# A 94-row table load becomes a 96-row load in a Fourier-mixing and MLP kernel

## The chip, the core and the metric

The kernel runs on one core of a Trainium2 chip. The metric is the device time of one execution in microseconds (us). The kernel before took 1952.17 us, the median of 8 runs (1951.83 to 1952.98). A profile is one further execution, with its own time and its own span (first to last recorded instruction).

## The reference

The input x has 8 sequences of 3008 rows and 256 columns. The reference takes the discrete Fourier transform over both axes, keeps the real part, and sends each of the 24064 rows through an MLP without biases:

```
X = fft(fft(x, axis=1), axis=2).real          # 8 x 3008 x 256
h = X.reshape(24064, 256) @ w_in              # w_in: 256 x 2048
g = h * clip(h + 3, 0, 6) / 6
out = g @ w_out                               # w_out: 2048 x 256, float32 throughout
```

## The kernel before, in words

3008 = 47 x 64, so the transform along a sequence is done in two stages (47 points, then 64), and the one along the columns is folded into the first weight matrix. The 8 sequences are taken as 4 pairs. For each pair, stage 1 reads x in eight tiles of four n2-columns, writes z to DRAM, and stage 2 reads it back transposed as g (load_g, L310). The MLP then runs over all (pair, chunk, step) triples, with the stages of the next pair put between its steps. The first pair has nothing to run beside, so its stage 1 is the head of the program, and this is where the change lies.

The head, in the order in which each engine meets it:

- TensorE (PE) is given nine dummy matmuls on zeros, keep_awake(9) (L669), each run as two, before anything else; then, tile by tile, stage 1 and one more keep_awake.
- The DMA queue of SyncE (SP) carries, one after the other, FI (L670: 128 rows of 33 numbers, row indices and a sign), F0 (L671: 94 rows of 6 x 96 numbers, the six tables of the first pair's stage 1; 94 = 2 x 47, the two sequences of the pair stacked), and CE (L679: 128 rows of two times 128 numbers). Later it carries C, T and the stores of z.
- VectorE (DVE) turns the indices of FI into integers (IX, L676). ScalarE (ACT) casts CE to the 16-bit E (L681) and then clears parts of T by two wide copies from Z (L688), before it copies the first z out of PSUM (L268, L279).
- GpSimd (POOL) issues the loads of x: load_forward (L154 and, for the first tile only, also L156) brings 96 rows in, load_partners (L175) gathers the rows in reversed order with IX. Each such pair of loads is 768 KB. Three tiles are loaded ahead (xpool holds two of them, spool one).
- fold (L180 to L201) adds and subtracts the two on DVE and writes y, which has two buffers. stage1_first (L253) multiplies y by the tables in F0 on PE: L261 and L263 into pt, L272, L275 and L278 into ps. ACT copies the results to z, and SP stores 16 rows of z at once (L285); the other rows are kept in the list later and are stored during the first chunk.

The eight tiles are taken in the order 7, 0, 1, ... 6 (ORDER). The load of tile k + 3 stands in GpSimd's program after the fold of tile k, whose buffers it takes over:

```
for c in ORDER[0:3]:
    load_x(first, c)
for k, c in enumerate(ORDER):
    for part in range(2):
        fold(first, c, part, nc.vector)
    stage1_first(first, c)
    keep_awake(1)
    if k + 3 < NXC:
        load_x(first, ORDER[k + 3])
```

Behind the last x load GpSimd issues the first four pieces of the weights (load_w, L555), and, once g has landed (see, L723), four more. From then on exponent_a (L574), exponent_b (L586), mantissa (L597, L598) and join rebuild the weights, fold_w_in (L635, L643) multiplies the first matrix by the column transform, and the MLP begins with mlp1 (L379). The program's order is written by hand (manual_schedule); semaphores between the engines follow from the tiles.

F0 is a tile of apool (tag "a", four buffers), the pool which later holds the MLP's activations a. The load of x for the first pair already has 96 rows where 94 are used (PR0 + 2, L153).

Of the kernel before, what the change touches and what calls it, by code (L numbers as in the profile page):

```python
# [7 lines left out]
F32 = mybir.dt.float32  # L8
# [50 lines left out]
def kernel(  # L59
# [10 lines left out]
    nc = tc.nc  # L70
# [8 lines left out]
    PB, PZ = P // 2, 2 * NK1  # L79
    PX = PB + N1 + 1  # L80
    PR0, PZ0 = 2 * N1, 2 * PZ
# [19 lines left out]
    apool = ctx.enter_context(tc.tile_pool(name="apool", bufs=4))  # L101
# [11 lines left out]
    ctx.enter_context(tc.manual_schedule())  # L113

    F = consts.tile([P, 5 * PB], F32, name="F")
    F0 = apool.tile([PR0, 6 * PZ0], F32, tag="a", name="F0")
    FI = consts.tile([P, NP * NXC + 1], F32, name="FI")
    IX = consts.tile([P, NP * NXC], I32, name="IX")
    T = consts.tile([P, 2, NG, 2, 2 * KK, N2], F32, name="T")
# [89 lines left out]
    def bank(shape, name):  # L209
        if starting[0]:  # L210
            return ps_a.tile(shape, F32, tag="acc", name=name)
        return ps_d.tile(shape, F32, tag="d", name=name)
# [40 lines left out]
    def stage1_first(pr, c):  # L253
        y = pr.y.pop(c)
        n = XC if c < NXC - 1 else XC - 1

        def table0(i):
            return F0[:, i * PZ0:(i + 1) * PZ0]

        pt = ps_h.tile([P, 2 * TB], F32, tag="uv", name="pt")[0:PZ0]  # L260
        nc.tensor.matmul(pt[:, 0:n], table0(5), y[:, 0:n, P], start=True, stop=True)  # L261
        for k in range(2 if n < XC else 0):
            nc.tensor.matmul(pt[:, n:XC], table0(k + 1), y[:, n + k, P:P + 1], start=(k == 0), stop=(k == 1))  # L263

        k = ORDER.index(c)
        pool, tag = (zpool, "z") if k < 2 else (cpool, "c") if k < 5 else (qpool, "q") if k < 7 else (apool, "a")
        z = pool.tile([PZ0, XC, D + 1], F32, tag=tag, name="z")
        nc.scalar.copy(z[:, :, D], pt[:, 0:XC])  # L268
        for i in range(XC // 2):
            ps = bank([P, 2, D], "ps1")[0:PZ0]  # L270
            if (c, i) == (NXC - 1, XC // 2 - 1):
                nc.tensor.matmul(ps[:, 0], table0(0), y[:, 2 * i], start=True, stop=False, skip_group_check=True)  # L272
                for k, (j, cs) in enumerate([(XC - 1, slice(0, P + 1)), (XC, slice(0, P + 1)),
                                             (XC - 1, slice(P + 1, D)), (XC, slice(P + 1, D))]):
                    nc.tensor.matmul(ps[:, 1, cs], table0(k + 1), y[:, j, cs], start=False, stop=(k % 2 == 1),  # L275
                                     skip_group_check=True)
            else:
                nc.tensor.matmul(ps, table0(0), y[:, 2 * i:2 * i + 2, :], start=True, stop=True)  # L278
            nc.scalar.copy(z[:, 2 * i:2 * i + 2, 0:D], ps)  # L279
        if pr.zd is None:  # L280
            pr.zd = dpool.tile([NG, 2, 2 * KK, 2, NS, D + 1], F32, tag="zd0", name="zd")
        zd = pr.zd[:].rearrange("g b k c n d -> (g b k c) n d")[:, c * XC:(c + 1) * XC, :]

        n0 = PZ0 // NG
        nc.sync.dma_start(out=zd[0:n0], in_=z[0:n0])  # L285
        later.append((zd[n0:], z[n0:]))
# [381 lines left out]
    nc.vector.memset(ones[:], 1.0)  # L668
    keep_awake(9)  # L669
    nc.sync.dma_start(out=FI[:], in_=c_stage1[:, 5 * PB + 6 * PZ0:])  # L670
    nc.sync.dma_start(out=F0[:], in_=c_stage1[0:PR0, 5 * PB:5 * PB + 6 * PZ0])  # L671
    bias = wpool.tile([P, 2], F32, tag="bias", name="bias")
    for i in range(2):
        nc.vector.memset(bias[:, i:i + 1], (2 * i - 1) * 7.5 / 16.0 - 896.0)
# [331 lines left out]
```

## Time and profile before

| | |
|---|---|
| median of 8 runs | 1952.17 us (1951.83 to 1952.98) |
| the profiled execution | 1952.85 us, of it span 1950.8 us |
| mean clock granted to PE | 0.999 of full speed |
| PE busy | 1929.1 us (99% of the span) |
| HBM | 57.57 MB read, 37.32 MB written |
| queue q0 (issued by POOL) | 36.67 MB, 6.7% of 16 DMA engines' span |
| queue q1 (issued by SP) | 58.05 MB, 12.5% of 16 DMA engines' span |

How to read it: "busy" is the time in which an engine had an instruction running. A line of the chain of waits gives when a piece of the chain that ended last began, how long it took and what it was: an instruction with its source line, or a DMA that something waited for. A line of the waits gives who waited for whom, the total in us, how often, and the longest. "DMA share" is the mean busy share of the core's 16 DMA engines: 1 is all of them working, 0.125 is two of them. "Landing" is when the instruction that waits for a transfer may go on.

### The profile page before, as it was taken

To read this page: it belongs to the slowest core of one execution; us is meant where nothing else is said; L and a number is where in the kernel's file an instruction comes from. 1 tells how busy PE (TensorE), PEld (TensorE's weight loads), DVE (VectorE), ACT (ScalarE), POOL (GpSimd) and SP (SyncE) were. 2 spreads that over 40 slices of the span, in tenths; PEclk is the share of its full clock that TensorE was granted. 3 is DMA by queue.
4 is the path that set the end of the run, shared out by engine and by line. 5 is a ranking of instruction groups with operands and counts; after the bars stand their busy time and mean duration, and the time that the engine had idled before them with its cause. 6 is when DMAs were issued, how large, how long until landed. Compare 5 with 4: busy or idle time off the path is not lost.

```text
span 1950.8 us, 27925 instructions
## 1 busy us (share of the span) xinstructions
PE 1929.1 (99%) x9254; PEld 1658.6 (85%) x9254; DVE 1438.9 (74%) x2777; ACT 681.9 (35%) x1167; POOL 1416.0 (73%) x1620
## 2 busy tenths in 40 slices
PE   8999999999999999999999999999999999999997
PEld 3678888888998888888898888888899888888887
DVE  6787767777777777777787777777778777777777
ACT  4633333333333333333333333333333333333332
POOL 3168888886678887787678887878667667666765
PEclk9999999999999999999999999999999999999999
DMA  7531222211112122121111221212110101101000
GB/s 212 181 80 49 71 54 58 57 39 35 34 32 55 44 68 70 42 55 28 41 34 44 58 56 42 51 50 54 35 28 20 28 17 26 35 13 28 19 19 20
DMA packets 148943, 96.71 MB, mean 50 GB/s; under 512 B 117777, under 2 KB 131221, under 8 KB 148798
## 3 DMA queue, kind: packets, MB, share of 16 engines
q1 hardware_dynamic: 137334, 58.05, 12.5%
q0 software_dynamic: 10672, 36.67, 6.7%
q8 instruction: 73, 1.20, 0.3%
q14 instruction: 72, 0.59, 0.1%
q10 hardware_dynamic: 792, 0.20, 0.0%
HBM read 57.57 MB, written 37.32 MB: 49 GB/s over the span
## 4 chain that ended last, share of the span: by engine, by line
PE 93%; DVE 3%; DMA 1%; ACT 1%; issue 1%; SPq 0%; DVEq 0%; POOL 0%; ACTq 0%; POOLq 0%
PE acc L464 56%; PE v L379 16%; PE u L379 16%; PE ps L328 2%; PE ps L223 1%; DMA xt<-in_x_dram,IX 1%; DVE a L424 1%; PE acc L448 1%; DVE s L384 1%; ACT t L421 1%; PE spare L635 0%; DVE o L522 0%; ACT PM L574 0%; DVE u L405 0%; DVE u L394 0%
## 5 line engine op out<-in xcount | busy, mean ns | idle before, releaser
L438 POOL TENSOR_TENSOR c<-a 128x512 f32<-128x512 f32 (+1 forms) x375 | 469.2, 1251 | 363.2 <-PE acc L464 299.4
L464 PE MATMUL acc<-c,G 128*128 128x256 f32 (+1 forms) x3008 | 696.9, 374 | 0.0
L421 ACT ACTIVATE t<-u,half 128x512 f32<-128x512 f32 (+1 forms) x384 | 260.6, 679 | 1143.6 <-DVE u L394 1064.5
L464 PEld LDWEIGHTS acc<-c,G 128*128 128x128 f32 x3008 | 565.4, 190 | 71.1
L384 DVE SCALAR_TENSOR_TENSOR s<-qn,WN,u 128x256 f32<-128x256 f32 (+1 forms) x768 | 330.4, 472 | 333.1 <-PE u L379 332.4
L464 PE MATMUL acc<-a,G 128*128 128x256 f32 (+1 forms) x2256 | 541.2, 375 | 0.0
L464 PEld LDWEIGHTS acc<-a,G 128*128 128x128 f32 x2256 | 421.3, 189 | 71.2 <-issue 17.5
L379 PE MATMUL v<-q,W 127*128 127x256 f32 (+1 forms) x1536 | 389.0, 375 | 2.4 <-DVE a L424 2.4
L379 PE MATMUL u<-q,W 128*128 128x256 f32 (+1 forms) x1536 | 388.1, 375 | 0.0
L424 DVE SCALAR_TENSOR_TENSOR a<-t,u 128x512 f32<-128x512 f32 (+2 forms) x448 | 263.9, 601 | 102.9 <-ACT t L421 98.9
L379 PEld LDWEIGHTS v<-q,W 127*128 127x128 f32 x1536 | 288.3, 190 | 42.2 <-DVE a L424 1.9
L379 PEld LDWEIGHTS u<-q,W 128*128 128x128 f32 x1536 | 285.7, 190 | 35.2 <-issue 0.5
L438 POOL TENSOR_TENSOR c<-a,c 128x256 f32<-128x256 f32 (+1 forms) x375 | 269.1, 718 | 29.4
L438 POOL TENSOR_TENSOR c<-c,a 128x256 f32<-128x256 f32 (+1 forms) x375 | 269.0, 717 | 29.4
L394 DVE TENSOR_TENSOR u<-s,v 128x512 f32<-128x512 f32 x352 | 245.0, 696 | 38.1 <-DVE s L384 1.8
L424 DVE SCALAR_TENSOR_TENSOR a<-t,v 128x512 f32<-128x512 f32 (+1 forms) x480 | 263.9, 566 | 0.2
L421 ACT ACTIVATE t<-v,half 128x512 f32<-128x512 f32 (+1 forms) x384 | 260.5, 678 | 0.6 <-PE acc L464 0.4
L396 DVE TENSOR_TENSOR v<-v,s 128x512 f32<-128x512 f32 x352 | 243.9, 693 | 0.0
L438 POOL TENSOR_TENSOR r<-w,e 128x256 f32<-128x256 f32 (+1 forms) x92 | 88.8, 987 | 3.6
L472 ACT ACTIVATE e<-acc 128x512 f32<-128x512 f32 (+2 forms) x186 | 84.3, 544 | 3.4 <-PE acc L464 3.3
L522 DVE STREAM_TRANSPOSE o<-r 128x256 f32<-128x256 f32 (+1 forms) x192 | 72.6, 415 | 0.2
L438 POOL TENSOR_TENSOR w<-w,e 128x512 f32<-128x512 f32 (+1 forms) x46 | 57.6, 1252 | 3.6
(104 smaller groups left out, 778.5 us busy)
## 6 DMA issues: line engine op xcount, KB each, us to landing
out_dram<-o SPq DMA_DIRECT2D x746, 32.0 KB
zd<-z SPq DMA_DIRECT2D x48, 192.0 KB
g<-zd SPq DMA_DIRECT2D x36, 256.0 KB
xt<-in_x_dram POOLq DMA_DIRECT2D x21, 256.0 KB
qn<-qd SPq DMA_DIRECT2D x19, 256.0 KB
st<-in_moe_w_in_dram POOLq DMA_DIRECT2D x8, 512.0 KB
st<-in_moe_w_out_dram POOLq DMA_DIRECT2D x8, 512.0 KB
xt<-in_x_dram POOLq DMA_DIRECT2D x17, 192.0 KB
```

Of the source, the lines that this page charges most:

```text
L223: nc.tensor.matmul(ps[b][h * PB:(h + 1) * PB, 0:n], F[rows(b), 0:PB], y[rows(b), 2 * h:2 * h + n], start=True, stop=not last, skip_group_c ...
L328: nc.tensor.matmul(ps[:, blk, u * P:n].rearrange("p (b k) -> p b k", b=2), g[:, kk, blk * (P + 1):blk * (P + 1) + P], T[:, :, gr, blk, kk, ...
L379: nc.tensor.matmul(ps[:, i, 0:nq], W1[r, blk, f * P:(f + 1) * P], q[r, blk, of:of + nq], start=True, stop=True)
L384: nc.vector.scalar_tensor_tensor(s[:, i, 0:nq], qn[:, of:of + nq], WN[:, f:f + 1], u[:, i, 0:nq], op0=AL.mult, op1=AL.add)
L394: nc.vector.tensor_tensor(u[:], s[:], v[:], op=AL.add)
L396: nc.vector.tensor_tensor(v[:], v[:], s[:], op=AL.subtract)
L421: nc.scalar.activation(t, h, AF.Relu, bias=half[:], scale=scale)
L424: nc.vector.scalar_tensor_tensor(dst, t, 1.0, h, op0=AL.min, op1=AL.mult)
L438: (eng or nc.gpsimd).tensor_tensor(out, in0, in1, op=AL.add)
L464: nc.tensor.matmul(ch.acc[i // 2][:, i % 2, 0:ch.n], G[:, i, fc, :], mv, start=(fc == 0 and i % 2 == 0), stop=(fc == NF - 1), skip_group_c ...
L472: nc.scalar.mul(ch.e[:, k:i + 1, 0:ch.n], ch.acc[i // 2][:, 0:i + 1 - k, 0:ch.n], 1.0 / WS)
L522: nc.vector.transpose(o[:, 0:n // DH, h], ch.r[:, m, h, 0:n].rearrange("p (j i) -> p j i", i=DH))
```

## The change

F0 gets two more rows, and its load brings two more rows of the same source (c_stage1 has 128 rows; rows 94 and 95 of this part are zeros). The matmuls go on using the first 94 rows.

```diff
-    F0 = apool.tile([PR0, 6 * PZ0], F32, tag="a", name="F0")
+    F0 = apool.tile([PR0 + 2, 6 * PZ0], F32, tag="a", name="F0")
...
         def table0(i):
-            return F0[:, i * PZ0:(i + 1) * PZ0]
+            return F0[0:PR0, i * PZ0:(i + 1) * PZ0]
...
-    nc.sync.dma_start(out=F0[:], in_=c_stage1[0:PR0, 5 * PB:5 * PB + 6 * PZ0])
+    nc.sync.dma_start(out=F0[:], in_=c_stage1[0:PR0 + 2, 5 * PB:5 * PB + 6 * PZ0])
```

PR0 is 94 and PZ0 is 96, so the transfer goes from 94 to 96 rows of 2304 bytes.

## The prediction

> **What bounds the kernel now.** I read the page first. The span is 1950.8 us, and TensorE is busy in almost all of it:
>
> ```profile
> PE 1929.1 (99%) x9254; PEld 1658.6 (85%) x9254; DVE 1438.9 (74%) x2777; ACT 681.9 (35%) x1167; POOL 1416.0 (73%) x1620
> ```
>
> A table that is loaded once, in the first 13 us, cannot change the matmul work. What it can change is when that work begins. So the second view is the chain that ended last, from 0 to 60 us, where each line is start, length and what ran:
>
> ```profile
> 3.00 9.31 DMA xt<-in_x_dram,IX
> ...
> 16.45 4.86 DMA xt<-in_x_dram,IX
> ...
> 25.22 7.45 DMA xt<-in_x_dram,IX
> ...
> 35.67 0.30 PE pt L261 x2
> ```
>
> Up to 32.7 us the end is set by the gathers of x (load_partners, L175), not by PE: the gather of the first tile lands at 12.31, that of the fourth at 21.31, that of the seventh at 32.68. After 35.67 the chain holds PE, ACT and DVE work and no DMA: from 60 to 400 us none is among its lines, and the page's chain gives DMA 1% of the span. So whatever the x loads win is handed on whole to the end.
>
> Third, the waits up to 25 us:
>
> ```profile
> ACT E L681 <- DMA CE<-in_c_dim_dram: 14.2, 1, 14.2
> DVE xt L187 <- DMA xt<-in_x_dram,IX: 8.8, 2, 8.1
> POOL xt L154 <- DVE y L201: 8.0, 1, 8.0
> ```
>
> VectorE stands 8.1 us for the first gather. GpSimd then stands until VectorE has folded that tile, because only then is a buffer free for load four. ScalarE waits 14.2 us, to 16.25, for CE, 128 KB issued 0.4 us behind F0 on the same queue.
>
> Fourth, the stretches of 1 us (time; length; busy PE, PEld, DVE, ACT, POOL; clock; DMA share; GB/s):
>
> ```profile
> 11.00:12.00 1.00, 1.00 (x4) 0.38 (x2) 0.00 (x0) 0.00 (x0) 0.00 (x0) 1.00 1.04 258
> 12.00:13.00 1.00, 0.54 (x2) 0.00 (x0) 0.58 (x2) 0.00 (x0) 0.00 (x0) 1.00 0.56 168
> 13.00:14.00 1.00, 0.00 (x0) 0.00 (x0) 0.97 (x2) 0.00 (x0) 0.00 (x0) 1.00 0.16 63
> 14.00:15.00 1.00, 0.11 (x2) 0.11 (x2) 1.00 (x5) 0.00 (x0) 0.00 (x0) 1.00 0.12 48
> 15.00:16.00 1.00, 0.78 (x7) 0.70 (x8) 1.00 (x6) 0.00 (x0) 0.39 (x1) 1.00 0.14 56
> 16.00:17.00 1.00, 1.00 (x4) 0.41 (x4) 0.97 (x2) 0.72 (x2) 0.69 (x2) 1.00 0.24 37
> 17.00:18.00 1.00, 1.00 (x10) 0.95 (x9) 1.00 (x4) 1.00 (x1) 0.39 (x1) 1.00 0.77 209
> ```
>
> A share near 0.125 is two engines of 16. From 13 to 16 us two DMA engines work alone while the rest have finished. The packet records of the trace say whose backlog it is: F0's 94 packets of 2304 bytes run in two streams from 2.17 to 12.79, and only two completions follow them, where FI (128 rows) has 16. Of CE's 256 packets 224 are done at 4.35; the other 32, on the same two engines, go out from 12.75 to 15.60. So F0 is carried by two engines, 108 KB each, and all that is queued on these two, a share of each x tile included, is late.
>
> **The change part by part.** The order of instructions is the same on all five engines but for one row: that DMA has 96 rows instead of 94. No wait or semaphore is added or moved; FI stays ahead of F0 on SP's queue and CE behind it. The matmuls read F0[0:94] as before, in the same shape.
>
> *Added.* Two packets of 2304 bytes, mean 0.152 us (14.28 us for 94): at most 0.3 us of one engine among 16, on no chain.
>
> *Spread.* If 96 rows go to 16 engines, each carries six packets, 6 x 0.152 = 0.9 us, or 6 x 0.092 = 0.55 us at the fastest rate in the records. No row of this trace shows 96 rows on SP's queue, only 128 and 16 (both with 16 completions), so I bound it: not spread, gain 0; spread, as follows. [...]
>
> *The first gather* (now 12.31). What has to move first is FI 16.5, F0 211.5, CE 128, the first tile 288 + 96 and its gather 384 KB: 1124 KB = 1.15 MB. The trace moved 146 GB/s x 7 us = 1.02 MB by 7.0 and then 271 GB/s, so 1.15 MB are through at 7.5. CE's wait ended 0.65 after its last packet: 8.1. If rings drift apart as the 14 free ones did then (the completions of this gather on them run from 6.3 to 7.6), 7.8 to 8.6. I take 8.1, 4.2 us earlier.
>
> [...] The row: from 2.0 to 3.2 us the hardware queue moved 138 packets and the x queue none, so F0 has about 1 us of nearly idle engines to itself. [...]
>
> *The fourth load.* Fold one takes 2.96 us (12.42 to 15.38): done at 11.1. GpSimd issues 0.23 later and first packets come 1.23 after that (15.61 to 16.84): 12.55. By then the three first loads, 2.72 MB with the tables, are nearly through: the trace had moved 198 GB/s x 12.5 = 2.48 MB by 12.5, and F0 uses the idle stretch before 3.2 for some 0.19 MB more. The rings run dry at 12.7 to 13.2, say 12.9, and the fourth load follows without a hole. Now its packets start at 16.84. Gain here: 3.95 us.
>
> *From there to the seventh gather* the DMA engines are the limit: from 16.8 to 32.7 they are 0.96 busy at 270 GB/s, moving 4.29 MB. The same bytes after 12.9 take the same time, less the two partial stretches at 17 to 18 and 19 to 20 us (0.77 and 0.75 busy, 0.48 us together, half of which I credit). So the seventh gather lands 3.95 + 0.25 = **4.2 us** earlier, at 28.5.
>
> *What is late next.* PE runs its 18 warming matmuls to 12.54 in either kernel, so it cannot begin earlier. From there tile one costs 3.77 us (14.89 to 18.88 without a stall of 0.22) and each further one 2.75 (23.27, 26.02, 28.77): tile seven could begin on PE at 12.54 + 3.77 + 5 x 2.75 = 30.1. By the data it begins at 28.5 + 2.99 (32.68 to 35.67) = 31.5, so the data still decide, by 1.4 us. VectorE writes y into two buffers, and fold three must wait for PE's tile one (15.6) some 0.7 us; load six is then issued at 17.2 and reaches the rings at 18.4, while loads four and five (1.57 MB at 0.27) keep them full to 18.7: covered. ScalarE casts E at about 5 instead of 16.27 and has the two 2.75 us copies into T behind it; the first z copy, at 22.10 now, and PE's stall of 1.38 before 22.31 go too, and both lie beside the DMA chain, so I count them at nothing.
>
> *Sum.* The profiled execution took 1952.85 (span 1950.8 and 2.05 around it): 1952.85 - 4.2 = 1948.65. It was 0.68 above the median of the eight runs (1952.17), so I forecast **1948.0**.
>
> **Rivals.**
> 1. *PE becomes the bound.* If the DMA engines drain x faster, the gain ends where PE does: 35.67 - 30.1 = 5.6 us, 1946.6. For it: from 35 to 36 us they moved 373 GB/s. Against it: from 17 to 28 us, with x tiles in most of the traffic, no microsecond went above 315.
> 2. *Only part of the hole closes.* Rings that finish at different times hold back each gather as the slowest of 16. Between the gathers of tiles six (26.9 at the latest, when its fold began) and seven (32.68) lie 5.8 us, though one load is 0.786 MB, 2.85 us at 0.276; C and four z stores (0.52 MB, 1.9 us) explain most of it, drift the other 1.0. If drift, now never reset by an idle stretch, takes 1.0 to 1.8 of the 4.2, the gain is 2.4 to 3.2: about 1949.4.
> 3. *It does not do what it says.* 96 rows stay on few engines, or the two streams were not F0's: 1952.2.
> 4. *Slower.* With ScalarE no longer held by CE, z stores and C start near 16 instead of 23.24 and run beside more of the x loads. If it is this mixing, not the bytes, that makes the 2.9 us of extra wait seen once before gather seven, it can strike loads five, six and seven: it decides from two further times on (5.8 - 4.2 = 1.6 slower, 1953.8), and at three costs 4.5, 1956.7. Against it: from 25 to 29 us, with the mixture, 280 GB/s, not less than without.
>
> **How the numbers follow.** Chances: the main case 0.60 (gain 3.4 to 5.0), PE bound 0.15 (5.0 to 5.8), part of the hole 0.15 (2.4 to 3.4), nothing 0.06, slower 0.04. The main case alone is 1947.2 to 1948.8. The range takes in the two neighbours, since their ends are those of the unknown costs: 1946.3 to 1949.8, leaving out 0.10. A measurement of this kernel tells a change from none at about 0.2%, 3.9 us; the forecast lies just beyond. Of the main case 0.41 lies beyond it, and with PE's 0.15 faster gets 0.56; slower by over 0.2% is half of rival four, 0.02; the rest, 0.42, is within.
>
> **What would show it.** The wait for CE should end near 5 instead of 16.25; the 8.1 us wait of VectorE should fall to about 3.9; DMA shares of 0.12 to 0.16 should be gone; the seventh gather should land near 28.5 and its tile start on PE near 31.5, at 30.1 for rival one. The step from there to the end should be as long as now. The forecast is wrong if F0 still runs in two streams, if gathers five to seven come more than 2.9 us apart, or if later waits give the start back.

## The result and the profile after

The changed kernel took 1948.05 us, the median of 12 runs (1947.60 to 1950.63); the kernel before, on the same chips, 1953.10 us (1951.28 to 1955.82, 32 runs). The ratio is 0.9975, with a 95% interval of 0.9968 to 0.9983: faster by 4.9 us, 3.3 to 6.2. The forecast was 1948.0, a gain of 4.2 from the 1952.17 of the first eight runs. The profiled execution of the changed kernel took 1949.14, its span 1947.4.

The waits up to 25 us, the same three as before (who waited for whom, total, times, longest):

```profile
DVE xt L187 <- DMA xt<-in_x_dram,IX: 5.0, 3, 3.8
...
POOL xt L154 <- DVE y L201: 3.8, 1, 3.8
ACT E L681 <- DMA CE<-in_c_dim_dram: 3.7, 1, 3.7
```

The longest wait of VectorE for a gather fell from 8.1 to 3.8 us, GpSimd's wait for that fold from 8.0 to 3.8, ScalarE's for CE from 14.2 to 3.7. VectorE begins the first fold at 8.20 instead of 12.42; CE is used at 5.73 instead of 16.27.

The stretches of 1 us (time; length; busy PE, PEld, DVE, ACT, POOL; clock; DMA share; GB/s):

```profile
12.00:13.00 1.00, 1.00 (x4) 0.47 (x4) 0.97 (x3) 0.16 (x1) 0.77 (x1) 1.00 0.99 160
13.00:14.00 1.00, 1.00 (x10) 0.90 (x9) 1.00 (x2) 0.58 (x1) 0.17 (x1) 1.00 0.72 266
14.00:15.00 1.00, 1.00 (x5) 0.51 (x4) 1.00 (x4) 0.58 (x1) 0.35 (x1) 1.00 0.88 188
15.00:16.00 1.00, 1.00 (x5) 0.50 (x4) 0.90 (x3) 0.16 (x1) 0.69 (x2) 1.00 0.69 262
16.00:17.00 1.00, 1.00 (x4) 0.45 (x3) 1.00 (x3) 0.58 (x1) 0.45 (x1) 1.00 0.81 123
```

Where two engines of 16 worked alone (shares of 0.12 to 0.24 from 13 to 17 us) the share is now 0.69 to 0.88: the hole is filled, not quite to the top. In the packet records of the trace F0's 96 packets run from 2.24 to 3.35, and 16 completions follow them, where 2 followed the 94.

The chain that ended last, 0 to 60 us:

```profile
4.88 6.70 DMA xt<-in_x_dram,IX
...
18.24 6.84 DMA xt<-in_x_dram,IX
...
28.08 0.30 PE pt L261 x2
28.38 2.21 PE ps L278 x4
30.59 1.71 PE awake L664 x2
32.30 0.17 PE pt L261 x2
```

It still runs through the x gathers, now the second and the sixth, up to 25.1 us. What follows was not in the forecast: from tile six on (28.08) the chain stays on PE, whose pieces are longer than they were (before: 1.79 for the four matmuls of ps, 0.87 for awake). The clock says why (stretches cut where it changes):

```profile
26.00:29.64 3.64, 1.95 (x7) 0.79 (x7) 2.95 (x6) 0.59 (x3) 1.55 (x3) 1.00 1.04 277
29.64:33.05 3.41, 3.41 (x7) 1.41 (x6) 2.80 (x6) 1.04 (x3) 0.00 (x0) 0.50 1.03 304
33.05:36.00 2.95, 2.95 (x10) 1.29 (x9) 2.40 (x6) 1.33 (x3) 0.00 (x0) 1.00 1.02 339
```

PE was granted half its clock for 3.41 us, after it had stood idle for 1.69 us before tile six:

```profile
25.80 0.59 PE L664 MATMUL awake<-Z,ones 128*128 128x512 f32 x1
28.08 0.30 PE L261 MATMUL pt<-y,F 94*96 94x4 f32 x2 [1.69 <-DVE y L195]
28.24 2.35 PE L278 MATMUL ps<-y,F 94*96 94x512 f32 x4
30.39 1.91 PE L664 MATMUL awake<-Z,ones 128*128 128x512 f32 x2
32.09 0.38 PE L261 MATMUL pt<-y,F 94*96 94x4 f32 x2
```

So tile seven began on PE at 32.09, though its y was there at 31.28. Two further profiles of the same kernel, below, have no such stretch. The first matmul of the MLP (u, L379), in the kernel before:

```profile
54.88 1.11 PE L379 MATMUL u<-q,W 128*128 128x256 f32 x4
```

and in the changed one:

```profile
51.50 1.11 PE L379 MATMUL u<-q,W 128*128 128x256 f32 x4
```

After this point nothing differs: to the end of the span it is 1895.9 us in both profiles of the kernel before (54.88 to 1950.8, 55.12 to 1951.0) and in all three of the changed one (51.50 to 1947.4, 49.74 to 1945.6, 50.00 to 1945.9), and 1895.8 to 1896.1 in the profiles of all the experiments. In the profiled executions all of the gain is made before 55 us and none is lost after it.

### The profile page after: what moved, and what is told of

Its sections match the earlier page's. It is cut to its first block, busy times and chain, and to the rows that moved or that the text cites. A ratio compares the mean times of both kernels' runs of the same rounds, so it can differ in the third digit from the quotient of the medians.

```text
span 1947.4 us, 27925 instructions
## 1 busy us (share of the span) xinstructions
PE 1929.2 (99%) x9254; PEld 1659.0 (85%) x9254; DVE 1439.1 (74%) x2777; ACT 682.6 (35%) x1167; POOL 1415.8 (73%) x1620
## 4 chain that ended last, share of the span: by engine, by line
PE 94%; DVE 3%; DMA 1%; ACT 1%; issue 0%; SPq 0%; POOL 0%; DVEq 0%; ACTq 0%
PE acc L464 56%; PE v L379 16%; PE u L379 16%; PE ps L328 2%; PE ps L223 1%; DVE a L424 1%; DMA xt<-in_x_dram,IX 1%; PE acc L448 1%; DVE s L384 1%; ACT t L421 1%; PE spare L635 0%; DVE o L522 0%; DVE u L405 0%; PE ps L278 0%; ACT PM L574 0%
## 5 line engine op out<-in xcount | busy, mean ns | idle before, releaser
L379 PE MATMUL v<-q,W 127*128 127x256 f32 (+1 forms) x1536 | 389.0, 375 | 2.3 <-DVE a L424 2.3
L379 PE MATMUL u<-q,W 128*128 128x256 f32 (+1 forms) x1536 | 388.1, 375 | 0.0
L379 PEld LDWEIGHTS v<-q,W 127*128 127x128 f32 x1536 | 288.3, 190 | 42.2 <-DVE a L424 1.9
L379 PEld LDWEIGHTS u<-q,W 128*128 128x128 f32 x1536 | 285.7, 190 | 35.2 <-issue 0.5
```

Of the source, the lines that this page charges most:

```text
L379: nc.tensor.matmul(ps[:, i, 0:nq], W1[r, blk, f * P:(f + 1) * P], q[r, blk, of:of + nq], start=True, stop=True)
```

## The experiments

My theory: 94 rows lie on two DMA engines; their backlog holds the first gather, and with it every later x load. The rivals: it is CE, stuck behind F0, that costs, through ScalarE; or two more rows matter as such. Three more questions came with the result: whether the half-clock stretch belongs to the change, what limits the changed kernel, and how much of the measured gain is clock.

**94 rows in two loads.**

```diff
-    nc.sync.dma_start(out=F0[:], in_=c_stage1[0:PR0, 5 * PB:5 * PB + 6 * PZ0])
+    for r in (slice(0, 80), slice(80, PR0)):
+        nc.sync.dma_start(out=F0[r], in_=c_stage1[r, 5 * PB:5 * PB + 6 * PZ0])
```

> 94 rows of F0 in two loads, rows 0 to 79 and rows 80 to 93, nothing else changed. Theory (94 rows sit on two DMA engines, and their backlog holds the first gather to 12.3 us): no two extra rows are needed; the wait for CE ends near 5.5, the first gather lands near 8.2, the time is that of the changed kernel, 3.5 to 5 us under the kernel before. Rival (the two extra rows matter as such, by a size or an alignment): the first gather stays near 12.3 and the time within 1 us of the kernel before.

Measured: 1949.00 (11 runs) against 1953.25, ratio 0.9980 (0.9971 to 0.9989); first fold at 8.25. The records show 16 completions for the 80 rows, 14 for the 14, and F0 through at 3.83. No extra row is needed; spreading is what counts. The changed kernel on the same chip (1947.68, below) was 1.3 us faster still, with intervals that overlap.

**CE ahead of F0**, still 94 rows.

```diff
-    nc.sync.dma_start(out=F0[:], ...)
...
     nc.sync.dma_start(out=CE[:], in_=dim[:, :, D:])
+    nc.sync.dma_start(out=F0[:], ...)
```

> 94 rows as before, but CE is issued ahead of F0. Theory: ScalarE's wait for CE ends by 4.5 instead of 16.25, while the two engines still carry F0, so the first gather stays at 12 to 12.6 and the time within 1 us of the kernel before. Rival (what costs is CE stuck behind F0, which holds ScalarE and through it the z copies and PE): most of the gain of the changed kernel appears, 3 us or more.

Measured: 1953.01 against 1953.25, ratio 0.9997 (0.9988 to 1.0006). Its waits up to 25 us, and two of its stretches of 1 us:

```profile
DVE xt L187 <- DMA xt<-in_x_dram,IX: 9.4, 3, 8.0
POOL xt L154 <- DVE y L201: 7.9, 1, 7.9
...
ACT E L681 <- DMA CE<-in_c_dim_dram: 1.6, 1, 1.6
```

```profile
13.00:14.00 1.00, 0.00 (x0) 0.00 (x0) 0.97 (x2) 0.00 (x0) 0.00 (x0) 1.00 0.14 52
14.00:15.00 1.00, 0.00 (x0) 0.00 (x0) 1.00 (x5) 0.00 (x0) 0.00 (x0) 1.00 0.12 50
```

ScalarE's wait, the longest of the old profile, went from 14.2 to 1.6 us and the time did not move; the gather still cost 8.0 and two engines still worked alone. The rival of CE is refuted.

**95 rows.**

```diff
-    F0 = apool.tile([PR0 + 2, 6 * PZ0], F32, tag="a", name="F0")
+    F0 = apool.tile([PR0 + 1, 6 * PZ0], F32, tag="a", name="F0")
...
-    nc.sync.dma_start(out=F0[:], in_=c_stage1[0:PR0 + 2, ...])
+    nc.sync.dma_start(out=F0[:], in_=c_stage1[0:PR0 + 1, ...])
```

> 95 rows instead of 94 or 96. If the number of DMA engines is the largest divisor of the rows up to 16, F0 lies on 5 engines, 19 packets each instead of 47 or 6: the first gather should land 1.2 to 2.0 us behind that of the changed kernel (13 packets more at 0.09 to 0.15 us), at 9.4 to 10.2, the gain over the kernel before 2.0 to 2.8 us. Rival (any rows above 94 do, or only multiples of 16): the full gain with a gather at 8.2, or none with a gather at 12.3.

Measured: first fold at 9.86, 1.7 us behind the changed kernel's, as expected of 5 engines; five completions of F0 in the records, its last packet at 5.28. Tile seven began on PE at 33.21, 2.5 us ahead of the kernel before, and the profiled execution took 1950.39, 2.5 less too. The timed runs gained more, 3.8 by the medians, 1949.44 against 1953.25, ratio 0.9979 (0.9970 to 0.9988, that is 2.3 to 5.9 us), so here the timing is above my range of 2.0 to 2.8 while the profile is inside it. It is still 1.8 us above the changed kernel's 1947.68 on the same chip. The five engines are shown by the completions and the gather, not by the timed gain.

Together, rows to engines by the completions in the records: 94 to 2, 95 to 5, 96 to 16, 80 to 16, 14 to 14. In these five cases, all on SP's queue, the number of engines is the largest divisor of the rows up to 16.

**The backlog put back**, in the changed kernel, by a load that nobody reads; **and its control** with 96 rows.

```diff
     nc.sync.dma_start(out=CE[:], in_=dim[:, :, D:])
+    extra = apool.tile([PR0, 6 * PZ0], F32, tag="a", name="extra")
+    nc.sync.dma_start(out=extra[:], in_=c_stage1[0:PR0, 5 * PB:5 * PB + 6 * PZ0])
```

> The changed kernel with one more load behind CE: 94 rows of the same table into a tile that nobody reads. F0 and CE are early as in the changed kernel; only a backlog of 108 KB on each of two DMA engines is back. Theory (that backlog alone holds the gathers): the first gather lands at 11.5 to 12.8 again, CE's wait still ends near 6, and the time goes back to that of the kernel before, within 1.2 us. Rival (what the change gained came from F0 or CE themselves being there earlier): gather near 8.2, time as the changed kernel plus at most 0.8 us.

> The same unread load with 96 rows, so 221 KB over 16 DMA engines: the control for the run before it. Theory: it costs its bytes, 0.22 MB at 0.27 MB per us: first gather 0.5 to 0.9 us later than in the changed kernel (8.7 to 9.1), time 0.3 to 1.0 us over the changed kernel. Rival (any extra load ahead of x costs the same, spread or not): as the 94-row one.

Measured, 94 rows: 1952.84 against 1953.32, ratio 0.9997 (0.9988 to 1.0006), first fold at 12.58. Its waits up to 25 us and two stretches:

```profile
DVE xt L187 <- DMA xt<-in_x_dram,IX: 8.7, 2, 8.1
POOL xt L154 <- DVE y L201: 8.0, 1, 8.0
...
ACT E L683 <- DMA CE<-in_c_dim_dram: 3.6, 1, 3.6
```

```profile
14.00:15.00 1.00, 0.00 (x0) 0.00 (x0) 1.00 (x4) 0.00 (x0) 0.00 (x0) 1.00 0.13 54
15.00:16.00 1.00, 0.74 (x7) 0.66 (x7) 0.53 (x4) 0.00 (x0) 0.24 (x1) 1.00 0.13 51
```

F0 and CE are as early as in the changed kernel, and yet the 8.1 us wait, the shares of 0.13 and the whole time are back. The backlog on two engines is enough by itself. With 96 rows the longest wait for a gather is half of that:

```profile
DVE xt L187 <- DMA xt<-in_x_dram,IX: 6.7, 4, 4.1
```

Here nearly the same bytes moved the first fold to 8.55 only (the changed kernel's three profiles: 8.20, 7.77, 8.21), and the time to 1949.91, ratio 0.9982 (0.9973 to 0.9991), a gain of 3.5: about 1.4 less than the changed kernel's 4.9, a little more than I allowed, with intervals that overlap. It is 2.9 us less than the 94-row load took on the same chip, so most of the cost is that of the two engines and not of the bytes.

**The changed kernel twice more**, unedited.

> The changed kernel once more, with a second profile. Theory: first gather 8.0 to 8.4, seventh 28.3 to 28.9, 3.5 to 5 us under the kernel before. Open: whether TensorE's granted clock drops to half near 30 us again, as it did in its first profile after 1.69 us without a matmul at 26.4. If the idle stretch causes it, it comes again whenever the sixth gather lands near 25.1; if it is chance, the clock stays at 1.00 and the span is some 0.8 us shorter.

> The changed kernel a third time, beside the three others on the same chip, for comparison and a third profile of the gathers. Expected: first gather 7.7 to 8.3, seventh 27.7 to 28.6, first matmul of the MLP at 49.5 to 51.6, the later end if the clock drops near 30 us.

Measured: 1947.68 (6 runs) against 1953.25, ratio 0.9971 (0.9958 to 0.9983), and 1947.58 (11 runs) against 1953.39, ratio 0.9974 (0.9965 to 0.9983). First folds at 7.77 and 8.21, seventh at 27.72 and 28.01; in neither does the clock drop, and tile seven begins on PE at 30.62 and 30.91. PE's idle stretches before tiles six and seven were 1.03 us in the one and 0.19 and 1.21 in the other. The first of the two beat its expectations (8.0 to 8.4, 28.3 to 28.9, and 3.5 to 5 us against the measured 5.6), the second kept to them. The stretch at half clock of the first profile is no fixed part of the change.

**The kernel before once more**, unedited.

> The kernel before once more, for a second profile. Theory: first gather at 12.1 to 12.6, the rings' shares near 0.12 from 13 to 16 us again. Open: whether the clock drops to half for a stretch of 3.41 us or a multiple after one of PE's idle stretches (before tiles one, three and seven); if so, this execution is longer than the first profile's by 0.8 to 1.8 us a stretch.

Measured: 1953.30 (11 runs), ratio to the others 1.0002 (0.9993 to 1.0011); first fold at 12.39, shares of 0.15, 0.14, 0.12 from 13 to 16 us. Here the clock drops in the old kernel:

```profile
13.00:14.00 1.00, 0.00 (x0) 0.00 (x0) 0.97 (x2) 0.00 (x0) 0.00 (x0) 1.00 0.15 59
14.00:15.00 1.00, 0.13 (x1) 0.14 (x2) 1.00 (x5) 0.00 (x0) 0.00 (x0) 0.92 0.14 56
15.00:16.00 1.00, 0.94 (x6) 0.85 (x6) 1.00 (x6) 0.00 (x0) 0.41 (x1) 0.50 0.12 49
```

PE ran at half clock from 14.85 to 21.67, after 3.79 us without a matmul before tile one. Yet tile seven begins at 35.99 against 35.67 without the drop, with its gather as much later (fold at 33.09 against 32.77), and the profiled execution took 1953.00 against 1952.85, not the 0.8 us or more longer that I expected: the waits for the gathers hide nearly all of it.

**Longer warming in the kernel before.**

```diff
-    keep_awake(9)
+    keep_awake(11)
```

> The kernel before (94 rows) with 11 warming matmul groups at the start instead of 9, so that PE runs on to about 14.3 us instead of 12.5 while it waits for the first tile at 14.9. Theory (part of what the change measures is not the DMA chain but half-clock stretches which PE's idle stretch before the first tile brings on in the kernel before; its runs had a mean granted clock of 0.997 against 0.9984): the mean clock rises to 0.998 or more and the time falls 0.5 to 1.3 us under the kernel before. Rival (the clock drops come from elsewhere): clock and time as the kernel before within 0.4 us.

Measured: 1953.12 against 1953.32, ratio 0.9999 (0.9990 to 1.0009). PE's idle time before tile one fell to 0.65 us, and the clock dropped all the same, from 17.43 to 20.84. So an idle stretch alone does not decide; in the 3.41 us before that drop PE mostly ran tile one's own matmuls, with idle stretches of 0.65 and 0.21. Drops of 3.41 us from about 17.0 on also stand in the profiles of CE ahead of F0 and of the backlog put back, after 3.14 and 2.91 us without a matmul, while the first profile of the kernel before has none after 2.35. My theory of the clock failed here, and what sets it off stays open.

**More warming in the changed kernel**, behind tiles five and six.

```diff
-        keep_awake(1)
+        keep_awake(2 if k in (4, 5) else 1)
```

> The changed kernel with two warming matmul groups instead of one behind tiles five and six, so that PE's wait for the sixth and seventh tile is filled (0.87 us more each). Theory (the drop of the clock comes from PE standing still for about half of one 3.41 us stretch of the clock, as in the changed kernel's first profile): no drop in the profile, PE's idle time before tiles six and seven under 0.9 us, time 0 to 1 us under the changed kernel, since only some of its runs have the drop. Rival (the idle stretch has nothing to do with it): the drop can show again, and the added 1.7 us of PE work cost up to 0.9 us.

Measured: no drop, and no idle time before tiles six and seven; 1948.41 against 1953.39, ratio 0.9979 (0.9970 to 0.9988), not better than the unedited kernel beside it (1947.58). The seventh gather happened to be late (fold at 28.45), so PE would have waited anyway.

**C and T behind the x tiles; and with half of the warming matmuls between tiles.**

```diff
         if k == 4:
             load_w(0)
             load_w(1)
-            load_t(0)
-        elif k == 1:
+        elif k == 6:
             nc.sync.dma_start(out=C[:], in_=dim[:, :, 0:D])
+            load_t(0)
```

The second kernel also has keep_awake(1 if k % 2 else 0) in place of keep_awake(1).

> The changed kernel with the loads of C and the first part of T issued behind the seventh tile's z store instead of behind the second and fifth. Theory (from 13 us on the DMA engines set the end, so bytes ahead of the seventh gather count): 0.52 MB less at 0.27 MB per us is 1.9 us; PE's own chain (10.97 + 3.54 + 5 x 2.75 = 28.3 for tile seven) then limits: tile seven on PE at 28.3 to 29.2 instead of 30.6 (or 32.1 with the clock drop), time 1.2 to 2.3 us under the changed kernel. Rival (drift between the rings or the gathers' own issue sets it): tile seven within 0.7 us of the changed kernel's, time the same within 0.7 us.

> As the run before it, and the warming matmuls only behind every second tile (four of eight). Theory: with C and T out of the way PE's chain is the limit; four of its pieces are 0.87 us shorter, so tile eight can begin up to 2.6 us sooner as far as the gathers allow (one each 2.85 us): 0.3 to 1.5 us under the run before it, unless PE's idle stretches halve the clock, which would cost 0.8 us or more. If the DMA engines are still the limit, no gain.

Measured: 1947.40, ratio 0.9972 (0.9961 to 0.9982), and 1947.39, ratio 0.9968 (0.9956 to 0.9980): not to be told from the changed kernel's 1947.58. In the first, tile seven began on PE at 30.28, only 0.3 to 0.6 ahead, and tile eight at 34.11, later than in the changed kernel (33.51 and 33.75). Its chain up to 32 us runs in rounds:

```profile
14.47 0.50 POOL xt L154
...
15.31 5.61 DMA xt<-in_x_dram,IX
...
24.07 0.54 POOL xt L154
...
24.90 6.28 DMA xt<-in_x_dram,IX
```

A load is issued when a fold frees its buffers and lands 6.4 to 7.1 us later, behind the loads issued before it. The 0.52 MB taken out of the way bought next to nothing, so the rival (how the single DMA engines finish and when loads are issued) comes nearer to these runs than my sum of bytes; what exactly limits the changed kernel's head stays open. In the second, PE stood idle for 1.34 and 1.25 us and the clock was at half from 26.72 to 33.55.

## Why the prediction was right

**Which engines carry F0.** Right: two streams before, 16 after. That 96 rows go to 16 engines was an assumption of mine, for no row of the profile of the kernel before shows it; in the changed kernel's records 16 completions follow the 96 packets. The unread 94-row load shows that the backlog on two engines is enough to bring the old time back, within its interval; the 96-row load and CE ahead of F0 show that the bytes do it only in small part and CE not at all.

**The first gather**: forecast 8.1 (7.8 to 8.6), 4.2 earlier; the fold, which begins 0.1 us after the landing, began at 8.20, 7.77 and 8.21 instead of 12.42 and 12.39, so one of the three was just earlier than the range. F0, which I gave about 1 us of nearly idle engines, was through at 3.4 to 3.6.

**The fourth load**: issue forecast at 11.3, found at 11.39; the hole closed, with shares of 0.69 to 0.99 from 12 to 17 us in place of 0.12 to 0.56. The forecast had it full from 12.9 on, so this step was taken a little too favourably.

**The seventh gather**: forecast 4.2 earlier, at 28.5. Its fold began at 28.52, 27.72 and 28.01, 4.3 to 5.1 us before the 32.77 (33.09 in the second profile of the kernel before). Mechanism right, size a little low. I credited 0.25 us for a smoother run from the fourth load on; the three profiles give up to 0.85 for all that I did not count. One sign of it: from the fourth load's packets to the seventh gather the old kernel moved 4.29 MB (16.8 to 32.7), the changed one 3.96 and 4.05 MB (12.9 to 27.7), so less was brought ahead of its turn. That is a reading of two windows, not an experiment.

**From there to the end**: forecast as long as before. From the start of the MLP on it is, to 0.1 us (1895.9).

**What late next**: the data were to decide tile seven on PE, at 31.5. They did in one of the profiles (30.91, after a wait of 1.21 us). In another (30.62) y was there at 30.48 and PE's warming ended at 30.55, nearly together, after PE had waited 1.03 us for tile six. In the first one PE decided, at 32.09, through the half clock, which I had not counted and which cost 0.8 us there. I also had PE's warming end at 12.54 in either kernel; it depends on when the clock rises (7.55 in the old profile, 5.74, 4.73 and 6.53 in the changed), and tile one could begin at 10.97 to 11.86. With 3.54 us for tile one instead of 3.77, rival one's limit of 30.1 for tile seven was therefore about 1 to 1.8 us too late in these executions.

**The sum.** 4.2 forecast, 4.9 measured (3.3 to 6.2): the forecast is inside. That the time itself, 1948.05, fell on the forecast 1948.0 is luck: the kernel before ran at 1953.10 in this comparison, 0.9 above the 1952.17 that the forecast started from, and the gain was larger by nearly as much. In the profiles the MLP began at 54.88 and 55.12 before and at 51.50, 49.74 and 50.00 after, 4.6 apart on average, with the half clock of the first in it.

How much half-clock stretches add to the gain of the timed runs stays open. Over 97 executions of the kernel before the mean granted clock was 0.9970, over 31 of the changed kernel 0.9984, and longer executions mostly go with a lower clock (before: median 1954.1 at 0.996, 1953.3 at 0.997, 1952.5 at 0.998, but 1953.5 for the two at 0.999). This mean is a poor measure of the head, though: it also counts a stretch at half clock at the end of the span, 4.2 to 7.4 us long in the 14 profiles, which comes behind the last matmul and costs nothing (the time from the MLP's start to the end stays at 1895.8 to 1896.1). By that alone two profiles of the changed kernel without a drop in the head have 0.999 and 0.998. The attempt to lift the old kernel's clock did not lift it, and the 6.83 us of half clock in its second profile went with an MLP that began only 0.24 us later.

**The rivals.** CE's wait, part of the main text as a thing that goes but counts nothing, did count nothing. "Nothing" is out, and partial filling (2.4 to 3.4) touches the measured interval only at its lower end. PE as the bound lies inside the interval by its number (5.0 to 5.8), but not by the profiles: at full clock PE's own pieces would have let tile seven begin at 28.3 (10.97 + 3.54 + 5 x 2.75) and 29.2, and it began at 30.62 and 30.91, since PE had waited for x. The slow rival did see its premise come true, z stores from 14.96 and C at 18.06, and gathers six and five drifted to 4.65 us apart (folds at 20.53 and 25.18), but the next came after 3.34, and from tile five to seven it was 7.99 us against 8.73 before. So my warning sign, gathers more than 2.9 us apart, was a bad one: the spacing of single gathers moved about while their sum held.

## What to carry to other kernels

Before a small load goes out ahead of the bulk, look at how many DMA engines carry it: count its completions, or look for a stretch in which the DMA share stays at the level of a few engines (0.12 to 0.16 here) while a transfer is waited for. The 94 rows cost twice here: the load itself was through at 12.8 us instead of 3.4, and the first fold, whose gather has a share on the same two engines, began at 12.42 instead of 8.20. And the longest wait of a profile (here ScalarE's 14.2 us) may be worth nothing, while a shorter one that gates the next issue (VectorE's 8.1 us, which fell by 4.3) was worth all that it fell by.

## What the runs showed of the hardware

- A load on SP's queue was carried by 2, 5, 16, 16 and 14 engines for 94, 95, 96, 80 and 14 rows, counted by its completions. With 94 rows of 2304 bytes the last packet was through at 12.8 us, with 96 at 3.4.
- A backlog of 47 packets of 2304 bytes on each of two of 16 engines held a 384 KB gather on another queue to about 12.4 us; without it the gather was there at about 8.2.
- PE's half-clock stretches in the head, after its first rise, were 3.41 us long or twice that (6.83), at places that differ between executions of one kernel. The clock dropped with a gap of 3.79 us without a matmul, but also with gaps of 1.69 and even 0.65, and did not with one of 2.35, so in these runs the length of the gap alone does not tell whether it drops.
